# Linear attention on one core: the orders of loads, stores and first and last heads, rewritten by hand

## The chip, the cores and the metric

The kernel runs on one core of one Trainium2 chip. The metric is the device time of one execution in microseconds (us). A kernel's time is the median of its runs. One execution more was taken with the hardware profiler; its span runs from the first to the last instruction on the core, and its device time is a little longer than that span.

## The reference

32 heads, each with q, k and v of 2048 rows by 128 columns in bf16. phi(x) is x + 1 where x > 0 and exp(x) elsewhere; the kernel computes it as max(x, 0) + min(exp(x), 1), with the small constant added to the second term.

```python
phi_q = jnp.where(q > 0, q + 1, jnp.exp(q)) + 1e-6
phi_k = jnp.where(k > 0, k + 1, jnp.exp(k)) + 1e-6
kv  = jnp.einsum("bhsd,bhse->bhde", phi_k, v)
z   = jnp.einsum("bhsd->bhd", phi_k)
num = jnp.einsum("bhqd,bhde->bhqe", phi_q, kv)
den = jnp.einsum("bhqd,bhd->bhq", phi_q, z)[..., None] + 1e-6
return num / den
```

q, k and v are 16.8 MB each and the output is as large again, so the core moves 67 MB through its DMA engines.

## The kernel before

**Tiles.** A head is loaded as three transfers of 512 KB (q, k, v) and stored as one of 512 KB. Row p*16 + j of a head lies in partition p at place j, so that each tensor of a head is a tile of 128 partitions by 16 blocks of 128 columns. There are 7 buffers for each of k, q and v (`NI`), 12 for the output (`NO`) and 2 for every intermediate tile.

**The steps of a head h, with the names that the order lists use.** A number after the dot is the part of a step that is cut (the first head's are cut in halves, the last head's q steps in three).

- `ldk`, `ldq`, `ldv` (lines 367 and 372): the loads. They are issued by SP, but for `ldv0.0`, which ScalarE issues. A load of head h waits until the tile of head h - 7 has been used.
- `ek` (L384, ScalarE): exp of k. `em` (L387, VectorE): its minimum with 1. `rkp` (L394, GpSimd) and for the first head `rkd` (L390, VectorE): max(k, 0). `v1` (L398, GpSimd): v copied beside a column of ones.
- `kv` (L405, TensorE): 32 matmuls that add up phi(k)^T [v, 1] in PSUM. `kvs` (L410, VectorE): the sum copied to SBUF.
- `T` (L417, TensorE): 16 transposes of q into PSUM. They need the PSUM tile free: `eq`, `rqa` and `rqb` of the head before.
- `eq` (L421) and `rqa` (L427) on ScalarE, `emq` (L423) and `rqb` (L430) on VectorE: phi of the transposed q.
- `n` (L441, L446, L448, TensorE): phi(q) times the copied sum, 12 blocks as `n.0` and 4 as `n.1` (6, 6 and 4 for the last head).
- `a` (L461), `r` (L464), `f` (L468, VectorE): the denominator plus its constant, its reciprocal, the product into the output tile. `f.0` is the big one, `f.1` the small one.
- `st` (L477, SP): the store, which waits for all `f` of its head. For the three heads in `FEW` (line 64) it is cut by rows instead: 96 partitions as an ordinary store (L351), the other 32 as pieces whose outermost dimension is 4 or 3 (L356).
- `w` (L339, TensorE): matmuls on the identity whose result nobody reads, 28 in all at the start.

**What sets the order.** Nothing is scheduled at run time. `ORDER` (line 105) lists for each of PE, DVE, ACT, POOL and SP the names of its steps in the order in which that engine runs them. `Program.resolve` turns the dependences into waits on semaphores. An engine does one step after the other, and a step that has to wait holds up everything behind it in its list. That holds for SP's list too: it is one line of loads and stores, all in one DMA queue, and a store whose `f` is not ready keeps the loads behind it from being issued.

In the line before, 25 loads of SP's list (places 0 to 24, counted from zero) stand ahead of the first store `st0.0`; with `ldv0.0` these are 26. From there on stores stand among the loads, and `st18.0` to `st31.2` stand behind the last load `ldq31.0`.

Of the kernel before, what the change touches and what calls it, by code (L numbers as in the profile page):

```python
# [57 lines left out]
def groups(h):  # L58
    if h == NH - 1:
        return ((0, 2, 3, 0), (6, 2, 3, 2), (12, 2, 2, 4))  # L60
    return ((0, 4, 3, 0), (12, 2, 2, 4))


FEW = {4: ((0, 96, 16), (96, 120, 3), (120, 128, 4)), 8: ((0, 96, 16), (96, 128, 4)), 17: ((0, 96, 16), (96, 128, 4))}


def st_rows(h, i):
    return FEW[h][i] if h in FEW else (0, P, 16)

# [34 lines left out]

ORDER = {
    "PE": """
        w16 w2 w0 w6 w7 kv0.0 w8 w5 T0.0 w9 w4 T0.1 w10 w11 w12 w13 w1 kv0.1 w14 w15 w3 T1.0 kv1.0 n0.0 n0.1
        T2.0 kv2.0 n1.0 T3.0 n1.1 kv3.0 n2.0 T4.0 n2.1 kv4.0 n3.0 T5.0 n3.1 kv5.0 n4.0 T6.0 n4.1 kv6.0 n5.0 T7.0
        n5.1 kv7.0 n6.0 T8.0 n6.1 kv8.0 n7.0 T9.0 n7.1 kv9.0 n8.0 T10.0 n8.1 kv10.0 n9.0 T11.0 n9.1 kv11.0 n10.0
        T12.0 n10.1 kv12.0 n11.0 T13.0 n11.1 kv13.0 n12.0 T14.0 n12.1 kv14.0 n13.0 T15.0 n13.1 kv15.0 n14.0  # L110
        T16.0 n14.1 kv16.0 n15.0 T17.0 n15.1 kv17.0 n16.0 T18.0 n16.1 kv18.0 n17.0 T19.0 n17.1 kv19.0 n18.0
        T20.0 n18.1 kv20.0 n19.0 T21.0 n19.1 kv21.0 n20.0 T22.0 n20.1 kv22.0 n21.0 T23.0 n21.1 kv23.0 n22.0
        T24.0 n22.1 kv24.0 n23.0 T25.0 n23.1 kv25.0 n24.0 T26.0 n24.1 kv26.0 n25.0 T27.0 n25.1 kv27.0 n26.0
        T28.0 n26.1 kv28.0 n27.0 T29.0 n27.1 kv29.0 n28.0 T30.0 n28.1 kv30.0 n29.0 T31.0 T31.1 n29.1 kv31.0
        n30.0 n30.1 n31.0 n31.1 n31.2
    """,
    "DVE": """
        ones eps0 em0.0 rkd0.0 v1ones0 em0.1 v1ones1 eps1 em1.0 emq0.0 rqb0.0 kvs0 emq0.1 eps2 em2.0 kvs1 rqb1.0
        r0.0 f0.0 emq1.0 em3.0 a0.1 kvs2 r0.1 rqb2.0 f0.1 r1.0 f1.0 emq2.0 em4.0 a1.1 r1.1 rqb3.0 f1.1 r2.0 kvs3
        f2.0 emq3.0 em5.0 a2.1 kvs4 r2.1 rqb4.0 f2.1 r3.0 f3.0 emq4.0 em6.0 a3.1 r3.1 rqb5.0 f3.1 r4.0 kvs5 f4.0  # L120
        emq5.0 em7.0 a4.1 r4.1 rqb6.0 f4.1 r5.0 kvs6 f5.0 emq6.0 em8.0 a5.1 r5.1 rqb7.0 f5.1 r6.0 kvs7 f6.0
        emq7.0 em9.0 a6.1 r6.1 rqb8.0 f6.1 r7.0 kvs8 f7.0 emq8.0 em10.0 a7.1 r7.1 rqb9.0 f7.1 r8.0 kvs9 f8.0
        emq9.0 em11.0 a8.1 r8.1 rqb10.0 f8.1 r9.0 kvs10 f9.0 emq10.0 em12.0 a9.1 r9.1 rqb11.0 f9.1 r10.0 kvs11
# [54 lines left out]
class Program:  # L178
# [84 lines left out]
def bass_standalone__linear_attn_elu__prompt_kernel(nc: bass.Bass, q: bass.AP, k: bass.AP, v: bass.AP, out: bass.AP):  # L263
# [11 lines left out]
    with ExitStack() as es:  # L275
# [99 lines left out]
        def head(h):  # L375
# [99 lines left out]
            for i, (a, b) in enumerate(st_parts(h)):  # L475
                add("SP", f"st{h}.{i}", lambda e, a=a, b=b, i=i: some(
                    e, o_sb[:, h % NO], of[h], *st_rows(h, i)) if h in FEW else e.dma_start(rows(of, h)[:, a:b], o_sb[:, h % NO, a:b]),  # L477
                    [f"f{h}.{j}" for j, (t0, nb, m, b0) in enumerate(groups(h)) if t0 < b and a < t0 + nb * m],
# [44 lines left out]
```

## Time and profile before

| What | Value |
|---|---|
| median of 3 runs | 169.07 us (168.45 to 169.11) |
| the profiled execution | 168.74 us |
| its span | 167.4 us |
| mean granted TensorE clock | 0.997 |
| TensorE, VectorE, ScalarE, GpSimd busy | 94%, 92%, 89%, 56% of the span |
| bytes read and written in HBM | 50.33 MB, 16.78 MB |

The table gives whole-span shares. The engines' shares are far from full only at both ends of the span; between 26 and 146 us TensorE, VectorE and ScalarE are all nearly without a gap, and so is the DMA.

### The profile page before, as it was taken

The numbers are of one execution on the slowest core, as the hardware profiler recorded it, in microseconds if no ns is written. First come the engines' busy times: TensorE is split into PE (matmuls) and PEld (weight loads), VectorE is DVE, ScalarE is ACT, GpSimd is POOL, SyncE is SP. The second block draws the span as 40 slices with busy tenths as digits, with TensorE's granted clock in tenths as the row PEclk, the third lists the DMA queues.
The fourth block names the chain that finished last, engine by engine and source line by source line (L and its number), as shares of the span: only waits on it lengthen the run. The fifth ranks groups of instructions, "written<-read, shape, count | busy, mean of one in ns | idle before, by whom it ended". The sixth has DMA issues, their size and how long they took to land.

```text
span 167.4 us, 6190 instructions
## 1 busy us (share of the span) xinstructions
PE 156.7 (94%) x2716; PEld 151.2 (90%) x2716; DVE 154.4 (92%) x300; ACT 149.5 (89%) x102; POOL 94.1 (56%) x71
## 2 busy tenths in 40 slices
PE   6999969999999999999999999999999999999740
PEld 2579859999999999999999999999999999999640
DVE  0389999999999999999999999999999999999990
ACT  4899949999999999999999999999999999995700
POOL 2779646656656666655555566666555555670000
PEclk9999999999999999999999999999999999999998
DMA  5999999999999999999999999999999999999995
GB/s 206 432 423 419 395 423 388 419 409 415 411 419 407 407 427 411 417 395 421 415 389 425 418 414 420 426 407 423 402 442 390 425 416 428 405 409 415 414 376 226
DMA packets 9834, 67.51 MB, mean 403 GB/s; under 512 B 2095, under 2 KB 2479, under 8 KB 6831
## 3 DMA queue, kind: packets, MB, share of 16 engines
q1 hardware_dynamic: 9663, 66.59, 97.3%
q8 instruction: 21, 0.34, 0.8%
q10 hardware_dynamic: 144, 0.52, 0.8%
q14 instruction: 6, 0.05, 0.1%
HBM read 50.33 MB, written 16.78 MB: 401 GB/s over the span
## 4 chain that ended last, share of the span: by engine, by line
PE 88%; DVE 8%; issue 0%; POOL 0%; POOLq 0%
PE la L405 34%; PE la L446 17%; PE la L417 17%; PE la L448 16%; PE la L339 5%; DVE la L468 4%; DVE la L387 1%; DVE la L423 1%; DVE la L464 1%; DVE la L430 0%; PE la L441 0%; DVE la L461 0%; DVE la L410 0%; POOL la L324 0%; POOL la L323 0%
## 5 line engine op out<-in xcount | busy, mean ns | idle before, releaser
L394 POOL TENSOR_SCALAR la<-la 128x2048 bf16<-128x2048 bf16 (+1 forms) x32 | 60.5, 1892 | 49.9 <-PE la L405 46.6
L468 DVE TENSOR_TENSOR la<-la 128x1536 bf16<-128x1536 f32 (+2 forms) x65 | 77.7, 1196 | 0.2
L446 PE MATMUL la<-la 128*128 128x129 bf16 x512 | 67.0, 219 | 0.1
L448 PE MATMUL la<-la 128*128 128x129 bf16 x512 | 67.0, 219 | 0.0
L421 ACT ACTIVATE la<-la 128x2048 bf16<-128x2048 bf16 (+2 forms) x35 | 60.2, 1730 | 5.3 <-PE la L448 4.0
L384 ACT ACTIVATE la<-la 128x2048 bf16<-128x2048 bf16 (+1 forms) x33 | 61.3, 1860 | 2.5 <-DMA la<-in_k_dram 2.5
L405 PE MATMUL la<-la 128*128 128x129 bf16 x1024 | 63.4, 220 | 0.0
L405 PEld LDWEIGHTS la<-la 128*128 128x128 bf16 x1024 | 59.5, 98 | 0.4
L448 PEld LDWEIGHTS la<-la 128*128 128x128 bf16 x512 | 49.5, 97 | 0.0
L446 PEld LDWEIGHTS la<-la 128*128 128x128 bf16 x512 | 47.9, 97 | 0.3 <-DVE la L410 0.3
L398 POOL COPY la<-la 128x1024 int32<-128x1024 int32 (+1 forms) x33 | 34.4, 1042 | 5.4 <-PE la L405 3.4
L417 PE MATMUL la<-la 128*128 128x128 bf16 x512 | 34.0, 219 | 1.6 <-DVE la L430 1.6
L427 ACT ACTIVATE la<-la 128x1024 bf16<-128x1024 bf16 (+1 forms) x32 | 33.5, 1047 | 0.0
L417 PEld LDWEIGHTS la<-la 128*128 128x128 bf16 x512 | 30.0, 98 | 2.4 <-DVE la L430 1.8
L387 DVE TENSOR_SCALAR la<-la 128x2048 bf16<-128x2048 bf16 (+1 forms) x33 | 24.8, 751 | 6.1 <-ACT la L384 6.1
L423 DVE TENSOR_SCALAR la<-la 128x2048 bf16<-128x2048 bf16 (+2 forms) x35 | 25.1, 717 | 0.3 <-ACT la L421 0.3
L441 PE MATMUL la<-la 128*128 128x3 bf16 (+1 forms) x128 | 21.6, 169 | 1.8 <-DVE la L468 1.4
L430 DVE TENSOR_SCALAR la<-la 128x1024 bf16<-128x1024 bf16 x31 | 20.5, 661 | 0.0
L441 PEld LDWEIGHTS la<-la 128*128 128x128 bf16 x128 | 12.5, 97 | 2.1 <-DVE la L468 1.5
L464 DVE RECIPROCAL la<-la 128x12 f32<-128x12 f32 (+2 forms) x65 | 12.9, 200 | 1.3 <-PE la L448 0.3
L339 PE MATMUL la<-la 128*128 128x480 bf16 x28 | 8.8, 464 | 1.5 <-POOL la L324 1.5
L410 DVE CAST la<-la 128x129 bf16<-128x129 f32 x32 | 7.8, 244 | 0.1
(16 smaller groups left out, 11.9 us busy)
## 6 DMA issues: line engine op xcount, KB each, us to landing
la<-in_k_dram SPq DMA_DIRECT2D x32, 512.0 KB, 19.2
la<-in_q_dram SPq DMA_DIRECT2D x32, 512.0 KB, 19.6
la<-in_v_dram SPq DMA_DIRECT2D x31, 512.0 KB, 19.4
out_dram<-la SPq DMA_DIRECT2D x28, 512.0 KB, 19.2
out_dram<-la SPq DMA_DIRECT2D x3, 384.0 KB
la<-in_v_dram ACTq DMA_DIRECT2D x1, 512.0 KB, 4.3
out_dram<-la SPq DMA_DIRECT2D x3, 128.0 KB, 3.8
out_dram<-la SPq DMA_DIRECT2D x2, 192.0 KB, 3.4
```

The costliest lines, as they stand in the source:

```text
L384: add("ACT", f"ek{h}.{i}", lambda e, a=a, b=b: e.activation(em_sb[:, h % NE, a:b], k_sb[:, h % NI, a:b], ACT.Exp), over("ldk", h, ld_parts ...
L394: add("POOL", f"rkp{h}.{i}", lambda e, a=a, b=b: e.tensor_scalar(rk_sb[:, h % NR, a:b], k_sb[:, h % NI, a:b], BIG, 0.0, op0=ALU.min, op1=A ...
L398: add("POOL", f"v1{h}.{i}", lambda e, a=a, b=b: e.tensor_copy(v1_sb[:, h % NV, a:b, 0:D].bitcast(i32), v_sb[:, h % NI, a:b].bitcast(i32)), ...
L405: ins = e.matmul(kv_ps, lhsT=src[:, j], rhs=v1_sb[:, h % NV, j, 0:NC], start=(j + part == 0), stop=(j == NT - 1 and part == 1))
L417: ins = e.transpose(xT[:, j], q_sb[:, h % NI, j], ident[:])
L421: add("ACT", f"eq{h}.{i}", lambda e, a=a, b=b: e.activation(emq_sb[:, h % NQ, a:b], xT[:, a:b], ACT.Exp), over("T", h, t_parts, a, b) + fr ...
L423: add("DVE", f"emq{h}.{i}", lambda e, a=a, b=b: e.tensor_scalar(emq_sb[:, h % NQ, a:b], emq_sb[:, h % NQ, a:b], 1.0, EPS, op0=ALU.min, op1 ...
L427: add("ACT", f"rqa{h}", lambda e: e.activation(rq_sb[:, h % NQ, 0:n], xT[:, 0:n], ACT.Relu), over("T", h, t_parts, 0, n) + freed(NQ, h, (" ...
L441: e.matmul(_ap(o_ps[:, :], o + D, [[NC, m]]), lhsT=ones[:], rhs=epsr[:, 0:m], start=True, stop=False, skip_group_check=True)
L446: e.matmul(to, lhsT=emq_sb[:, h % NQ, t], rhs=kvs_sb[:, h % NK, 0:NC], start=late and c == 0, stop=False, skip_group_check=True)
L448: ins = e.matmul(to, lhsT=rq_sb[:, h % NQ, t], rhs=kvs_sb[:, h % NK, 0:NC], start=False, stop=True, skip_group_check=True)
L468: return e.tensor_tensor(out=_ap(o_sb[:, :, :, :], first(o_sb[:, h % NO, t0, 0:1]) - first(o_sb[:, :, :, :]), [[m * D, nb], [D, m], [1, D] ...
```

## The change

Only `FEW` and the lists in `ORDER` are edited. Every step stays, with its size and its engine; the waits between steps are worked out anew from the new order.

- **SP.** `ldq5.0` and `ldk6.0` change places, and `st0.0` now stands at place 18, right behind 18 loads. Stores then stand among the loads at an even pace. Where before `st0` to `st17` stood ahead of the last load, now `st0` to `st20` do, and 11 stores stand behind it where there were 14.
- **Pieces.** The stores cut by rows are those of heads 0, 2 and 5 instead of 4, 8 and 17. The cuts are the same: one head in 96 + 24 + 8 partitions, two heads in 96 + 32.
- **TensorE.** At the start 22 `w` matmuls stand ahead of `T0.0`, one between `T0.0` and `T0.1`, then both halves of `kv0`, then 5 more `w`. At the end `kv31.0` stands ahead of `n29.1`, `T31.0` and `T31.1`.
- **VectorE.** Some small steps of the first heads move (`emq1.0` goes ahead of `f0.0`; `kvs2` and `kvs4` come later), and the last six heads are ordered anew (`emq29.0` behind `f28.0`, `rqb30.0` behind `f28.1`, `emq30.0` behind `f29.0`, the parts of `emq31` and `kvs31`).
- **ScalarE.** `rqa30` goes ahead of `eq30.0`, and `rqa31` ahead of `eq31.2`.
- **GpSimd.** `rkp27.0` goes ahead of `v127.0`, `v128.0` ahead of `rkp28.0`, `rkp29.0` ahead of `v129.0`.

```diff
-FEW = {4: ((0, 96, 16), (96, 120, 3), (120, 128, 4)), 8: ((0, 96, 16), (96, 128, 4)), 17: ((0, 96, 16), (96, 128, 4))}
+FEW = {0: ((0, 96, 16), (96, 128, 4)), 2: ((0, 96, 16), (96, 128, 4)), 5: ((0, 96, 16), (96, 120, 3), (120, 128, 4))}
...
     "PE": """
-        w16 w2 w0 w6 w7 kv0.0 w8 w5 T0.0 w9 w4 T0.1 w10 w11 w12 w13 w1 kv0.1 w14 w15 w3 T1.0 kv1.0 n0.0 n0.1
+        w16 w5 w6 w7 w2 w8 w4 w9 w1 w0 w10 T0.0 w11 T0.1 kv0.0 kv0.1 w12 w13 w3 w14 w15 T1.0 kv1.0 n0.0 n0.1
...
-        T28.0 n26.1 kv28.0 n27.0 T29.0 n27.1 kv29.0 n28.0 T30.0 n28.1 kv30.0 n29.0 T31.0 T31.1 n29.1 kv31.0
+        T28.0 n26.1 kv28.0 n27.0 T29.0 n27.1 kv29.0 n28.0 T30.0 n28.1 kv30.0 n29.0 kv31.0 n29.1 T31.0 T31.1
         n30.0 n30.1 n31.0 n31.1 n31.2
     "DVE": """
-        ones eps0 em0.0 rkd0.0 v1ones0 em0.1 v1ones1 eps1 em1.0 emq0.0 rqb0.0 kvs0 emq0.1 eps2 em2.0 kvs1 rqb1.0
-        r0.0 f0.0 emq1.0 em3.0 a0.1 kvs2 r0.1 rqb2.0 f0.1 r1.0 f1.0 emq2.0 em4.0 a1.1 r1.1 rqb3.0 f1.1 r2.0 kvs3
-        f2.0 emq3.0 em5.0 a2.1 kvs4 r2.1 rqb4.0 f2.1 r3.0 f3.0 emq4.0 em6.0 a3.1 r3.1 rqb5.0 f3.1 r4.0 kvs5 f4.0
+        ones rkd0.0 em0.0 eps0 v1ones0 v1ones1 em0.1 em1.0 emq0.0 eps1 rqb0.0 kvs0 emq0.1 eps2 em2.0 kvs1 rqb1.0
+        r0.0 emq1.0 f0.0 em3.0 a0.1 r0.1 rqb2.0 f0.1 r1.0 kvs2 f1.0 emq2.0 em4.0 a1.1 r1.1 rqb3.0 f1.1 r2.0 kvs3
+        f2.0 emq3.0 em5.0 a2.1 r2.1 rqb4.0 f2.1 r3.0 kvs4 f3.0 emq4.0 em6.0 a3.1 r3.1 rqb5.0 f3.1 r4.0 kvs5 f4.0
...
-        f24.0 emq25.0 em27.0 a24.1 r24.1 rqb26.0 f24.1 r25.0 kvs26 f25.0 emq26.0 em28.0 a25.1 r25.1 rqb27.0
-        f25.1 r26.0 kvs27 f26.0 emq27.0 em29.0 a26.1 r26.1 rqb28.0 f26.1 r27.0 kvs28 f27.0 emq28.0 em30.0 a27.1
-        r27.1 rqb29.0 f27.1 kvs29 r28.0 emq29.0 f28.0 em31.0 a28.1 rqb30.0 r28.1 kvs30 f28.1 r29.0 emq30.0 f29.0
-        emq31.0 a29.1 r29.1 f29.1 emq31.1 kvs31 r30.0 emq31.2 f30.0 a30.1 r30.1 f30.1 r31.0 f31.0 a31.1 r31.1
-        r31.2 f31.1 f31.2
+        f24.0 emq25.0 em27.0 a24.1 r24.1 rqb26.0 f24.1 r25.0 kvs26 f25.0 emq26.0 em28.0 a25.1 kvs27 r25.1
+        rqb27.0 f25.1 r26.0 f26.0 emq27.0 em29.0 a26.1 r26.1 rqb28.0 f26.1 r27.0 kvs28 f27.0 emq28.0 em30.0
+        a27.1 r27.1 rqb29.0 f27.1 r28.0 kvs29 f28.0 emq29.0 em31.0 a28.1 r28.1 kvs30 f28.1 rqb30.0 r29.0 f29.0
+        emq30.0 a29.1 kvs31 r29.1 f29.1 emq31.0 emq31.1 r30.0 f30.0 a30.1 r30.1 emq31.2 f30.1 r31.0 f31.0 a31.1
+        r31.1 r31.2 f31.1 f31.2
     "ACT": """
...
-        eq30.0 rqa30 eq31.0 eq31.1 eq31.2 rqa31
+        rqa30 eq30.0 eq31.0 eq31.1 rqa31 eq31.2
     "POOL": """
...
-        rkp21.0 v121.0 rkp22.0 v122.0 rkp23.0 v123.0 rkp24.0 v124.0 rkp25.0 v125.0 rkp26.0 v126.0 v127.0 rkp27.0
-        rkp28.0 v128.0 v129.0 rkp29.0 rkp30.0 v130.0 rkp31.0 v131.0
+        rkp21.0 v121.0 rkp22.0 v122.0 rkp23.0 v123.0 rkp24.0 v124.0 rkp25.0 v125.0 rkp26.0 v126.0 rkp27.0 v127.0
+        v128.0 rkp28.0 rkp29.0 v129.0 rkp30.0 v130.0 rkp31.0 v131.0
     "SP": """
         ldk0.0 ldk1.0 ldq0.0 ldv1.0 ldk2.0 ldq1.0 ldv2.0 ldk3.0 ldq2.0 ldv3.0 ldk4.0 ldq3.0 ldv4.0 ldq4.0 ldk5.0
-        ldv5.0 ldk6.0 ldq5.0 ldv6.0 ldk7.0 ldv7.0 ldv8.0 ldq6.0 ldk8.0 ldq7.0 st0.0 ldv9.0 ldk9.0 ldq8.0 ldv10.0
-        ldk10.0 st1.0 ldk11.0 ldq9.0 ldk12.0 ldq10.0 ldk13.0 ldv11.0 ldq11.0 ldv12.0 ldq12.0 st2.0 ldv13.0
-        ldv14.0 st3.0 ldv15.0 ldk14.0 ldq13.0 st4.0 ldq14.0 ldk15.0 st4.1 ldv16.0 ldk16.0 ldk17.0 ldq15.0
...
-        ldv27.0 st12.0 ldq27.0 ldv28.0 ldk28.0 st13.0 ldv29.0 ldq28.0 ldk29.0 st14.0 ldq29.0 ldk30.0 st15.0
-        ldv30.0 ldk31.0 ldq30.0 st16.0 ldv31.0 st17.0 st17.1 ldq31.0 st18.0 st19.0 st20.0 st21.0 st22.0 st23.0
+        ldv5.0 ldq5.0 ldk6.0 st0.0 ldv6.0 ldk7.0 ldk8.0 ldq6.0 ldv7.0 st0.1 ldq7.0 ldv8.0 ldq8.0 ldk9.0 ldv9.0
+        st1.0 ldk10.0 ldk11.0 ldv10.0 ldq9.0 st2.0 ldv11.0 ldq10.0 ldk12.0 ldv12.0 ldq11.0 st2.1 ldq12.0 ldv13.0
+        ldk13.0 ldv14.0 ldk14.0 st3.0 ldv15.0 ldq13.0 ldv16.0 ldk15.0 st4.0 ldq14.0 ldk16.0 ldk17.0 st5.0
+        ldq15.0 st5.1 ldq16.0 st5.2 ldv17.0 ldq17.0 ldk18.0 ldq18.0 ldv18.0 st6.0 ldk19.0 ldv19.0 ldq19.0
...
+        st12.0 ldq26.0 st13.0 ldv27.0 ldk28.0 ldv28.0 ldq27.0 st14.0 ldq28.0 st15.0 ldk29.0 ldv29.0 ldk30.0
+        ldv30.0 ldq29.0 st16.0 st17.0 ldk31.0 ldq30.0 ldv31.0 st18.0 st19.0 st20.0 ldq31.0 st21.0 st22.0 st23.0
         st24.0 st25.0 st26.0 st27.0 st28.0 st29.0 st30.0 st31.0 st31.1 st31.2
```

More of the change, by code (lines that the diff above doesn't have):

```diff
@@ L155 @@
         ldk0.0 ldk1.0 ldq0.0 ldv1.0 ldk2.0 ldq1.0 ldv2.0 ldk3.0 ldq2.0 ldv3.0 ldk4.0 ldq3.0 ldv4.0 ldq4.0 ldk5.0
-        ldv5.0 ldk6.0 ldq5.0 ldv6.0 ldk7.0 ldv7.0 ldv8.0 ldq6.0 ldk8.0 ldq7.0 st0.0 ldv9.0 ldk9.0 ldq8.0 ldv10.0
-        ldk10.0 st1.0 ldk11.0 ldq9.0 ldk12.0 ldq10.0 ldk13.0 ldv11.0 ldq11.0 ldv12.0 ldq12.0 st2.0 ldv13.0
-        ldv14.0 st3.0 ldv15.0 ldk14.0 ldq13.0 st4.0 ldq14.0 ldk15.0 st4.1 ldv16.0 ldk16.0 ldk17.0 ldq15.0
-        ldk18.0 ldq16.0 ldq17.0 ldv17.0 ldk19.0 st4.2 ldq18.0 ldq19.0 ldv18.0 ldv19.0 ldk20.0 st5.0 ldv20.0
-        ldk21.0 st6.0 ldq20.0 ldk22.0 ldq21.0 ldv21.0 ldk23.0 st7.0 ldv22.0 ldk24.0 st8.0 ldq22.0 ldv23.0 st8.1
-        ldv24.0 ldv25.0 ldq23.0 st9.0 ldq24.0 ldq25.0 ldk25.0 st10.0 ldk26.0 ldk27.0 ldq26.0 st11.0 ldv26.0
-        ldv27.0 st12.0 ldq27.0 ldv28.0 ldk28.0 st13.0 ldv29.0 ldq28.0 ldk29.0 st14.0 ldq29.0 ldk30.0 st15.0
-        ldv30.0 ldk31.0 ldq30.0 st16.0 ldv31.0 st17.0 st17.1 ldq31.0 st18.0 st19.0 st20.0 st21.0 st22.0 st23.0
+        ldv5.0 ldq5.0 ldk6.0 st0.0 ldv6.0 ldk7.0 ldk8.0 ldq6.0 ldv7.0 st0.1 ldq7.0 ldv8.0 ldq8.0 ldk9.0 ldv9.0
+        st1.0 ldk10.0 ldk11.0 ldv10.0 ldq9.0 st2.0 ldv11.0 ldq10.0 ldk12.0 ldv12.0 ldq11.0 st2.1 ldq12.0 ldv13.0
+        ldk13.0 ldv14.0 ldk14.0 st3.0 ldv15.0 ldq13.0 ldv16.0 ldk15.0 st4.0 ldq14.0 ldk16.0 ldk17.0 st5.0
+        ldq15.0 st5.1 ldq16.0 st5.2 ldv17.0 ldq17.0 ldk18.0 ldq18.0 ldv18.0 st6.0 ldk19.0 ldv19.0 ldq19.0
+        ldk20.0 st7.0 ldv20.0 ldq20.0 ldk21.0 ldk22.0 st8.0 ldv21.0 ldk23.0 ldq21.0 ldv22.0 st9.0 ldv23.0
+        ldq22.0 ldq23.0 ldq24.0 st10.0 ldk24.0 ldv24.0 ldk25.0 ldk26.0 st11.0 ldv25.0 ldq25.0 ldk27.0 ldv26.0
+        st12.0 ldq26.0 st13.0 ldv27.0 ldk28.0 ldv28.0 ldq27.0 st14.0 ldq28.0 st15.0 ldk29.0 ldv29.0 ldk30.0
+        ldv30.0 ldq29.0 st16.0 st17.0 ldk31.0 ldq30.0 ldv31.0 st18.0 st19.0 st20.0 ldq31.0 st21.0 st22.0 st23.0
         st24.0 st25.0 st26.0 st27.0 st28.0 st29.0 st30.0 st31.0 st31.1 st31.2
```

## The prediction

> **What bounds the kernel now.** I read the page first, then busy time by stretches, the waits, the chain of work that ended last, and the timelines of SP and VectorE at both ends. The page, in shares of the span:
>
> ```profile
> span 167.4 us, 6190 instructions
> ...
> DMA  5999999999999999999999999999999999999995
> ...
> q1 hardware_dynamic: 9663, 66.59, 97.3%
> ```
>
> The queue of loads and stores alone fills 97.3% of the 16 DMA engines' time, and only the first and the last slice are not full. By stretches (busy time per engine, granted clock, DMA share, GB/s):
>
> ```profile
> 4.00:26.00 22.00, 20.03 (x280) 16.58 (x279) 18.02 (x27) 18.70 (x14) 14.71 (x11) 1.00 1.02 416
> 26.00:58.00 32.00, 32.00 (x585) 31.97 (x583) 31.76 (x64) 31.75 (x22) 20.69 (x14) 1.00 1.01 410
> 58.00:90.00 32.00, 32.00 (x586) 32.00 (x583) 31.76 (x64) 31.78 (x22) 20.13 (x14) 1.00 1.02 414
> 90.00:130.00 40.00, 40.00 (x732) 40.00 (x730) 39.69 (x81) 39.75 (x27) 24.66 (x18) 1.00 1.01 416
> 130.00:146.00 16.00, 16.00 (x294) 16.00 (x292) 15.90 (x31) 15.88 (x11) 9.89 (x7) 1.00 1.01 416
> 146.00:160.00 14.00, 12.49 (x227) 12.15 (x225) 13.55 (x31) 10.13 (x9) 3.33 (x2) 1.00 1.01 410
> 160.00:167.00 7.00, 1.67 (x32) 1.50 (x29) 3.53 (x8) 0.00 (x0) 0.00 (x0) 0.97 0.79 313
> ```
>
> The DMA runs at 410 to 416 GB/s from 4 to 160 us, whether only loads are in it (4 to 26), loads and stores, or almost only stores (146 to 160). One transfer of 512 KB (524288 bytes) takes 524288/414 = 1.27 us at that rate. From 26 to 146 TensorE, VectorE and ScalarE are full too. Here the waits from 26 to 150 us, all of them, and two steps of the chain:
>
> ```profile
> POOL la L394 <- PE la L405: 44.9, 25, 3.5
> POOL la L398 <- PE la L405: 3.4, 2, 1.7
> ACT la L421 <- PE la L448: 2.2, 1, 2.2
> ```
>
> ```profile
> 140.32 1.81 PE la L405 x32
> ...
> 144.94 1.81 PE la L405 x32
> ```
>
> Nobody waits for a load; a head takes 144.94 - 140.32 = 4.62 us on TensorE. Two things thus run side by side, the compute at its own pace and the DMA at its own, and which of them ends last is seen at the end: SP's last four stores, and what SP waited for after 160 us.
>
> ```profile
> 160.56 3.40 SPq L477 DMA_DIRECT2D out_dram<-la  x4
> ```
>
> ```profile
> SPq L494 <- DMA out_dram<-la: 3.1, 2, 2.2
> ```
>
> The last store is issued at 163.96 and the span ends 3.4 us later. How long would it take if nothing were queued ahead of it? The first load went into an empty queue:
>
> ```profile
> 0.73 0.40 SPq L372 DMA_DIRECT2D la<-in_k_dram  x1
> ...
> 3.97 2.00 ACT L384 ACTIVATE la<-la 128x1024 bf16<-128x1024 bf16 x2 [1.74 <-DMA la<-in_k_dram]
> ```
>
> From issue to use are 3.24 us for 512 KB. The last store is 128 KB, so three quarters of 1.27 us go: 2.3 us. The other 1.1 us are transfers still queued. **The DMA bounds the end, and the compute may end up to 1.1 us later for nothing.** An earlier end of compute gains at most what the DMA leaves idle.
>
> **The change part by part.** Bytes, transfers and cuts of pieces stay, so the DMA's busy time stays. It can end earlier or later only if it idles less or more, or if the compute passes it by over 1.1 us.
>
> *Does the queue run dry at `st0.0`?* SP around it:
>
> ```profile
> 15.85 0.65 SPq L367 DMA_DIRECT2D la<-in_q_dram  x1
> 23.83 0.35 SPq L477 DMA_DIRECT2D out_dram<-la  x1
> 24.23 0.94 SPq L367 DMA_DIRECT2D la<-in_v_dram  x1
> ```
>
> SP stands until 23.83, when `f0.1` is done. Before, 26 loads are queued then; after, 19. At 4.0 one has landed; 416 GB/s over 22 us are 9.15 MB or 17.5 more, 18.5 by 26.0, so the nineteenth ends at 26.0 + 0.5 x 1.27 = 26.6. A store issued into an empty queue needs 3.24 - 1.27 = 2.0 us around its transfer; issued by 24.6 it follows without a hole. `f0.1` leaves 0.8 us. Behind it SP issues loads in at most 0.94 us each, less than 1.27, so the queue fills again. Cost: nothing, covered by the queued loads. Is `f0.1` still as early?
>
> ```profile
> 18.48 1.51 DVE L423 TENSOR_SCALAR la<-la 128x2048 bf16<-128x2048 bf16 x1
> 19.90 2.37 DVE L387 TENSOR_SCALAR la<-la 128x2048 bf16<-128x2048 bf16 x1
> ...
> 22.27 0.28 DVE L410 CAST la<-la 128x129 bf16<-128x129 f32 x1
> ...
> 22.55 0.66 DVE L430 TENSOR_SCALAR la<-la 128x1024 bf16<-128x1024 bf16 x1
> 23.13 0.68 DVE L468 TENSOR_TENSOR la<-la 128x512 bf16<-128x512 f32 x1
> ```
>
> These are `emq1.0`, `em3.0`, `kvs2`, `rqb2.0`, `f0.1`; the page's groups give the means of the lines of `em` and of `rqa`:
>
> ```profile
> L427 ACT ACTIVATE la<-la 128x1024 bf16<-128x1024 bf16 (+1 forms) x32 | 33.5, 1047 | 0.0
> L387 DVE TENSOR_SCALAR la<-la 128x2048 bf16<-128x2048 bf16 (+1 forms) x33 | 24.8, 751 | 6.1 <-ACT la L384 6.1
> ```
>
> After, `emq1.0` and `f0.0` swap, their sum stays, and `kvs2` leaves the way of `rqb2.0`: all behind it is 22.55 - 22.27 = 0.2 to 0.3 us earlier, and `T3.0`, which needs `rqb2.0`, with it. The unknown is how long the bf16 steps take at this place: `em3.0` has 2.37 us here and a mean of 0.75, and `emq1.0`, as large, has 1.51. So `f0.1` lies between 1.6 us earlier (`em3.0` at its mean) and 0.9 later (`emq1.0` as long as `em3.0`). I take 0.2 earlier, nearest to the row as it stands.
>
> *The first heads on TensorE.* The same 28 `w` and the same 96 transposes and matmuls of heads 0 and 1 stand ahead of `n0.0`, in another order. I take 0; a stall of up to 0.5 us would be under the same cover of 1.1.
>
> *Do the loads still come in time?* Now three more stores stand ahead of `ldq31.0`: it is transfer 117 in units of 512 KB (96 loads, 21 stores), before 114. The stretches add up to 1 + 17.5 + 25.0 + 25.3 + 31.7 + 12.7 = 113.2 by 146.0, so it lands at 146.0 + 3.8 x 1.28 = 150.9 on an average DMA engine, 3.8 later than before. It is used by `T31.0`:
>
> ```profile
> 152.83 0.89 PE la L417 x16
> 154.18 1.83 PE la L405 x32
> ```
>
> The first row is `T31`, the second `kv31`; the 0.46 between them is `n29.1`. After, `kv31` and `n29.1` stand ahead of `T31`: 152.83 + 1.83 + 0.46 = 155.1. Slack 4.2. The other tight loads by the same sum, `ldv29.0` (transfer 105), `ldk31.0` (111), `ldq30.0` (112) and `ldv31.0` (113), land at 135.7, 143.2, 144.5 and 145.8 on average. Their uses, `v129`, `rkp31`, `T30` and `v131`, in the same order, with `rkp29` second:
>
> ```profile
> 137.58 1.04 POOL L398 COPY la<-la 128x1024 int32<-128x1024 int32 x1 [1.72 <-PE la L405]
> 138.58 1.89 POOL L394 TENSOR_SCALAR la<-la 128x2048 bf16<-128x2048 bf16 x1
> ...
> 146.84 1.89 POOL L394 TENSOR_SCALAR la<-la 128x2048 bf16<-128x2048 bf16 x1 [1.74 <-PE la L405]
> 148.68 1.49 POOL L398 COPY la<-la 128x1024 int32<-128x1024 int32 x1
> ```
>
> ```profile
> 148.21 0.89 PE la L417 x16
> ```
>
> Slacks are 1.9, 3.6, 3.7 and 2.9. But `rkp29` goes ahead of `v129` now, so `v129` starts at 137.58 + 1.89 = 139.5, and `kv29` wants it only at 144.94. A load counts when its slowest DMA engine is done, and this lag shows where somebody waited for a load:
>
> ```profile
> 18.40 1.04 POOL L398 COPY la<-la 128x1024 int32<-128x1024 int32 x1 [1.22 <-DMA la<-in_v_dram]
> ```
>
> `ldv3.0` is the eleventh transfer, on average at 16.6 by the sum; it was used at 18.4: lag 1.8 us. The slacks, 2.9 and more, cover that. Cost: nothing.
>
> *The tail on VectorE.* From `f29.0` on:
>
> ```profile
> 153.68 1.74 DVE L468 TENSOR_TENSOR la<-la 128x1536 bf16<-128x1536 f32 x1
> ...
> 156.03 0.16 DVE L461 TENSOR_SCALAR la<-la 128x4 f32<-128x4 f32 x1 [0.28 <-PE la L405]
> ...
> 157.78 1.75 DVE L468 TENSOR_TENSOR la<-la 128x1536 bf16<-128x1536 f32 x1
> ```
>
> From `f29.0` (153.68) to the last `f` VectorE has one gap, 0.28 at `a29.1`, which waits for `kv31`. After, `kv31` is 1.4 earlier and the gap goes; `emq31.2` moves behind `f30.0`, as `rqa31` (2048 wide, some 1.9 where 1024 take 1.05) now runs ahead of `eq31.2`: +0.15 on the last `f`. Net between -0.3 and +0.3, I take 0; hidden by 1.1.
>
> **Sum:** span 167.4 + 0 (dry queue) + 0 (loads) + 0 (compute -0.2 at the start and 0 in the tail, both hidden) = 167.4. The profiled execution took 168.74, 1.3 more than its span, and lies 0.33 below the median 169.07. Forecast 168.7, its own range 168.0 to 169.4.
>
> **The rivals.** A measurement here can tell about 0.5% (0.85 us) from no change.
>
> *Late loads (slower).* Pieces with an outermost dimension of 4 or 3 cannot use all 16 DMA engines alike. Were they always to fall on the same few, those carry 8 + 8 + 8 rows from the pieces and 2 more by head 5's last one, 26 above the others, by place 60 instead of place 115. A row of 4 KB at 414/16 GB/s takes 0.158 us, so they end 4.1 us behind, and with the 1.8 measured 5.9. Then `ldq30.0` lands at 144.5 + 5.9 = 150.4, 2.2 after its use; less 1.1 of cover the end moves by 1.1: **169.8**. It decides from a lag of 3.7 + 1.1 = 4.8 on. For it: the DMA share of 0.79 in the last 7 us, some engines ending earlier than others. Against it: the same pieces were all in the queue by then before, too, and nobody waited. The Trainium skill, "DMA: Bandwidth & Descriptors", section "Why a DMA increments its semaphore by 16 and not by 1", says that the engine count is the largest number up to 16 that divides the slowest dimensions, and that hardware queues use the lowest-numbered ones; by that rule the same few it is, whereas no row here shows which engine took what.
>
> *Dry queue (slower).* If `f0.1` comes 0.9 later, 24.7, the hole is 0.1; if another 1.5 comes on top (`emq1.0` doubled), 1.6: up to 170.3; the middle is **169.6**.
>
> *Filled tail (faster).* 0.21 x 7 = 1.5 us of an average engine's time is idle in the last stretch. If the new order fed those engines earlier, up to 1.5 would go; two thirds of it give **167.7**. Against it: VectorE's last `f` is no earlier by more than some tenths.
>
> *No effect of the order at all*, that is, SP standing at the stores as long as before for want of room in the queue, gives the forecast's time.
>
> **How the numbers follow.** Forecast, with the last rival: 0.56. Late loads 0.20, dry queue 0.08, filled tail 0.16. Faster 0.16, same 0.56, slower 0.28. The range reaches to both neighbours: from 167.7 (the filled tail) to 170.2 (late loads with 0.4 more lag).
>
> **What would show it.** Right: DMA slices full from the second to the last but one, `st0.0` issued at 23.3 to 24.0, no wait for a load after 26 us, the last store's issue within 0.4 of 163.96. Late loads: ScalarE, GpSimd or TensorE waiting for a DMA after 100 us, and an end of compute beyond 165. Dry queue: a DMA slice at 26 to 30 us below 9. The forecast is wrong if the GB/s between 26 and 146 move, since it takes them as fixed.

## The result, and the profile after

| What | Before | After |
|---|---|---|
| median | 168.93 us (16 runs, 168.45 to 169.22) | 168.28 us (16 runs, 168.17 to 169.02) |
| the profiled execution, its span | 168.74, 167.4 us | 168.94, 167.6 us |
| profiled once more (`after_again` below) | | 168.25, 166.9 us |

The ratio after to before is 0.9972 [0.9958, 0.9985]: a gain of 0.3%. Its interval does not reach 1, but it lies inside the half per cent that the prediction counted as no change.

The first profiled execution of after lies 0.66 us above its own median. Its span, DMA slices and queue, from its page of the profile:

```profile
span 167.6 us, 6190 instructions
...
DMA  5999999999999999999999999999999999999995
...
q1 hardware_dynamic: 9663, 66.59, 96.9%
```

Two stretches show where (in each row: the stretch and its length, busy time of PE, PEld, DVE, ACT and POOL, granted clock, DMA share, GB/s; a share of 1.01 is read as full):

```profile
4.00:26.00 22.00, 21.23 (x316) 18.22 (x315) 17.24 (x33) 20.44 (x16) 15.07 (x12) 1.00 1.02 406
26.00:90.00 64.00, 63.64 (x1156) 63.44 (x1154) 63.55 (x124) 63.01 (x42) 40.37 (x28) 1.00 1.01 415
```

Its first 22 us, with only loads in the queue, ran at 406 GB/s where before had 416: 10/416 of 22 us, 0.5 us lost before any store. The second profiled execution of the same kernel started at 415, so that is no property of the change. I therefore read the second one, by the stretches that the prediction used:

```profile
4.00:26.00 22.00, 22.00 (x324) 18.93 (x323) 17.99 (x34) 21.06 (x16) 16.20 (x12) 1.00 1.02 415
26.00:58.00 32.00, 32.00 (x585) 32.00 (x583) 31.76 (x64) 31.77 (x22) 20.54 (x15) 1.00 1.01 414
58.00:90.00 32.00, 31.78 (x574) 31.49 (x572) 31.37 (x63) 31.22 (x21) 19.21 (x15) 1.00 1.01 415
90.00:130.00 40.00, 40.00 (x730) 40.00 (x728) 39.72 (x78) 39.72 (x27) 25.57 (x18) 1.00 1.01 417
130.00:146.00 16.00, 15.92 (x290) 15.75 (x288) 15.86 (x32) 15.65 (x11) 9.43 (x7) 1.00 1.02 421
146.00:160.00 14.00, 12.21 (x222) 11.89 (x219) 13.70 (x29) 8.57 (x8) 2.53 (x2) 1.00 1.00 405
160.00:167.00 7.00, 0.38 (x8) 0.20 (x5) 2.27 (x6) 0.00 (x0) 0.00 (x0) 0.71 0.73 287
```

Against before's rows in the prediction the DMA is faster in four stretches: 414 for 410, 415 for 414, 417 for 416, 421 for 416. Times their lengths these are (4 x 32 + 1 x 32 + 1 x 40 + 5 x 16) KB = 0.28 MB, or 0.68 us at 414 GB/s; the slower first stretch takes back 1 x 22 KB. At 146 us after is thus 0.6 us of transfers ahead. From 146 to 160 us it is slower, 405 for 410 at a share of 1.00, which takes back 5 x 14 = 70 KB or 0.2 us; in the last stretch less is left to do. That leaves some 0.45 us, and the spans differ by 0.5. Up to 146 us the DMA share is as full as before, 1.01 to 1.02: no idle time was filled, **the transfers themselves were faster**.

SP's stores at the end, its first store, and the waits for loads from 26 to 150 us (waited in total, times, longest):

```profile
159.32 3.35 SPq L477 DMA_DIRECT2D out_dram<-la  x4
```

```profile
21.47 0.37 SPq L351 DMA_DIRECT2D out_dram<-la  x1
```

```profile
POOL la L394 <- DMA la<-in_k_dram: 8.8, 4, 2.9
POOL la L398 <- DMA la<-in_v_dram: 1.1, 3, 0.5
```

The last store is issued at 162.67, 1.3 earlier than before, and 4.2 us pass to the end of the span instead of 3.4. The first store is issued 2.4 us earlier. And GpSimd now does wait for loads, 9.9 us in all, where before nobody did.

### The profile page after: what moved, and what is told of

The parts are those of the page before. It is cut to its first block, busy times and chain, and to the rows that moved or that the text cites. A ratio compares the mean times of both kernels' runs of the same rounds, so it can differ in the third digit from the quotient of the medians.

```text
span 167.6 us, 6190 instructions
## 1 busy us (share of the span) xinstructions
PE 156.3 (93%) x2716; PEld 150.9 (90%) x2716; DVE 153.6 (92%) x300; ACT 149.5 (89%) x102; POOL 93.9 (56%) x71
## 4 chain that ended last, share of the span: by engine, by line
DVE 80%; PE 11%; DMA 4%; issue 2%; SPq 1%
DVE la L468 40%; DVE la L423 11%; DVE la L387 10%; DVE la L430 10%; DVE la L464 5%; PE la L405 4%; DMA la<-in_q_dram 4%; DVE la L410 3%; PE la L417 2%; DVE la L461 2%; PE la L446 2%; PE la L448 2%; PE la L339 1%; SPq L367 0%; SPq L372 0%
## 5 line engine op out<-in xcount | busy, mean ns | idle before, releaser
L387 DVE TENSOR_SCALAR la<-la 128x2048 bf16<-128x2048 bf16 (+1 forms) x33 | 23.3, 705 | 4.1 <-ACT la L384 4.0
L423 DVE TENSOR_SCALAR la<-la 128x2048 bf16<-128x2048 bf16 (+2 forms) x35 | 26.1, 745 | 0.0
L339 PE MATMUL la<-la 128*128 128x480 bf16 x28 | 7.9, 440 | 1.5 <-POOL la L324 1.5
```

The lines of the kernel that those rows point to most:

```text
L387: add("DVE", f"em{h}.{i}", lambda e, a=a, b=b: e.tensor_scalar(em_sb[:, h % NE, a:b], em_sb[:, h % NE, a:b], 1.0, EPS, op0=ALU.min, op1=AL ...
L423: add("DVE", f"emq{h}.{i}", lambda e, a=a, b=b: e.tensor_scalar(emq_sb[:, h % NQ, a:b], emq_sb[:, h % NQ, a:b], 1.0, EPS, op0=ALU.min, op1 ...
```

## The experiments

Three theories stood at the start; the expectations number them. **DMA** (theory 1): only what is in the one queue, and when, counts. **Compute** (theory 2): the new orders of the heads end the compute earlier or later, and that is the time. **Pieces** (theory 3): the new places of the cut stores make the gain. All ratios are to the kernel before, with their 95% intervals; spans, stretches and rows are of the one profiled execution of each.

**compute_new.** Before, with the changed lists of TensorE, VectorE, ScalarE and GpSimd; SP's line and `FEW` stay.

```diff
 FEW, "SP": as before
-"PE", "DVE", "ACT", "POOL": as before
+"PE", "DVE", "ACT", "POOL": as after
```

> The kernel before with the changed kernel's lists for TensorE, VectorE, ScalarE and GpSimd; SP's line and the pieces stay as before. Theory 1 (the DMA line sets the end, the order of the compute is hidden): ratio to before 1.000, within 0.1%, although the compute ends earlier. Theory 2 (the compute, ahead by 1.6 us at head 5 in the changed kernel's profile, hands the last stores over earlier and fills the tail): 0.997. Theory 3 (the places of the pieces): 1.000.

1.0001 [0.9982, 1.0019]. SP's stores at its end:

```profile
155.01 7.75 SPq L477 DMA_DIRECT2D out_dram<-la  x5
```

The last store goes out at 162.76, 1.2 us earlier than before, and the span is 167.7: nothing is gained. An earlier end of the compute is worth nothing while before's line of transfers stays, as theory 1 had it.

**sp_new.** The other half: before, with after's SP line and `FEW`.

```diff
-FEW, "SP": as before
+FEW, "SP": as after
 "PE", "DVE", "ACT", "POOL": as before
```

> The kernel before with the changed kernel's line for SP and its pieces (heads 0, 2 and 5); the compute lists stay as before. Theory 1 (the new line of loads and stores alone makes the gain): 0.997. Theory 2 (the earlier compute makes it): 1.000, or slower by up to 0.5%, as the last loads come later for an order of steps that wants them earlier. Theory 3 (the places of the pieces): 0.997.

0.9987 [0.9967, 1.0006], between before and after and told apart from neither, so the time decides between no two theories. The stretch from 26 to 90 us, first of before, then of sp_new, and sp_new's stores at the end:

```profile
26.00:90.00 64.00, 64.00 (x1167) 63.97 (x1165) 63.52 (x126) 63.53 (x43) 40.82 (x28) 1.00 1.01 412
```

```profile
26.00:90.00 64.00, 63.84 (x1159) 63.61 (x1157) 63.28 (x125) 63.12 (x42) 39.17 (x29) 1.00 1.01 415
```

```profile
154.35 10.73 SPq L477 DMA_DIRECT2D out_dram<-la  x6
```

The DMA is as fast as in after, 415 where before has 412, but the last store is issued only at 165.08, 2.3 us from the end. That is the time estimated for a last store with nothing queued ahead of it: here the compute ends last.

**pieces_old, no_pieces, pieces_late, pieces_012.** After, with the cut stores at heads 4, 8, 17; with none; at heads 16, 17, 18; at heads 0, 1, 2. The pieces' places in SP's line go with them. Two more theories come in with the last two expectations. Theory R: pieces put the DMA engines out of step, so that some store while others load, and packets of loads get shorter by that. Theory L: the new line alone makes the gain. In these diffs C2 stands for ((0, 96, 16), (96, 128, 4)) and C3 for ((0, 96, 16), (96, 120, 3), (120, 128, 4)).

```diff
-FEW = {0: C2, 2: C2, 5: C3}
+FEW = {4: C3, 8: C2, 17: C2}     # pieces_old
+FEW = {}                         # no_pieces
+FEW = {16: C2, 17: C2, 18: C3}   # pieces_late
+FEW = {0: C2, 1: C2, 2: C3}      # pieces_012
```

> The changed kernel with its pieces back at heads 4, 8 and 17 (the same cuts, at such places of the new line that they follow their heads as before). Theory 3 (early pieces make the gain): the gain goes, 1.000. Theories 1 and 2: it stays, 0.997.

> The changed kernel with whole stores only, no piece anywhere. If the last DMA engines set the end and the pieces take rows off them, this is slower than the changed kernel: 26 rows of 0.158 us on the few against 6 fewer on each of the others, so about 6 x 0.158 = 0.9 us or 0.5%: ratio to before 1.002 to 1.003. If the compute sets the end, it stays at 0.997.

> The changed kernel with the same three cuts at heads 16, 17 and 18, the last before the last load. Rows of each DMA engine in all are those of the changed kernel. Theory R: the gain goes, 0.2 to 0.3% slower than the changed kernel, 0.999 to 1.001, with 26 to 90 us at the rate of the kernel without pieces. Theory L, or only the sum of rows of each engine counts: 0.997.

> The changed kernel with the same three cuts at heads 0, 1 and 2, the earliest possible. Theory R: as fast as the changed kernel or 0.1% faster, 0.996 to 0.997, with 26 to 58 us at 415 GB/s or more. Theory L: 0.997. If the changed kernel's own three heads were a lucky fit to the instruction fetches: slower, 1.000.

1.0006 [0.9985, 1.0028], 1.0055 [1.0038, 1.0072], 1.0022 [1.001, 1.0035] and 0.9984 [0.9971, 0.9996]. The stretch from 26 to 90 us of each, in this order:

```profile
26.00:90.00 64.00, 63.54 (x1156) 63.40 (x1153) 63.02 (x124) 62.94 (x42) 39.52 (x28) 1.00 1.01 413
```

```profile
26.00:90.00 64.00, 62.24 (x1122) 61.65 (x1120) 62.23 (x120) 61.14 (x41) 39.19 (x28) 1.00 1.01 411
```

```profile
26.00:90.00 64.00, 63.15 (x1149) 63.00 (x1147) 62.62 (x122) 62.55 (x41) 39.35 (x28) 1.00 1.01 412
```

```profile
26.00:90.00 64.00, 63.53 (x1142) 62.78 (x1140) 62.84 (x122) 62.27 (x41) 40.23 (x28) 1.00 1.01 415
```

With the new line alone nothing is gained, against theory L; with early pieces the rate is 415 and the time falls. The pieces count twice: where they stand, and that they are there at all (0.8% between none and after). Two sizes were missed: no pieces cost twice what was expected (1.002 to 1.003), and pieces_012 gained half (0.996 to 0.997). Why is not shown.

**early_in_old.** Before's line and compute, only the pieces at heads 0, 2, 5.

```diff
-FEW = {4: C3, 8: C2, 17: C2}
+FEW = {0: C2, 2: C2, 5: C3}
 "SP": loads and st*.0 as before
```

> The kernel before with one thing changed: its pieces are of heads 0, 2 and 5, each placed in the old line a few transfers behind its head's store. Theory R (pieces put the DMA engines out of step, so that some store while others load, and load packets get shorter; the earlier, the longer this works): ratio to before 0.998, and the GB/s from 26 to 90 us rise by 2 or 3. Theory L (the new line, with stores from place 18 on, makes the gain, the pieces none): 1.000.

0.9994 [0.9985, 1.0003]: no change that can be told.

```profile
26.00:90.00 64.00, 64.00 (x1168) 64.00 (x1165) 63.51 (x126) 63.57 (x42) 39.56 (x29) 1.00 1.01 412
```

Pieces of early heads alone do not raise the rate either. But in the old line they are not as early in time. The pieces' rows (L356: shortest, median and longest ns at SP, first and last start), early_in_old, then after_again:

```profile
L356 SPq DMA_DIRECT2D out_dram<-la x4: 792/1122/2118, 23.5 to 76.4; - x4
```

```profile
L356 SPq DMA_DIRECT2D out_dram<-la x4: 790/942/1083, 25.3 to 60.0; - x4
```

The last piece goes out 16 us later than in after_again. So it takes both parts of the change as they are; that the new line does more than bring the pieces forward is not shown.

**dry.** After, with `st0.0` ahead of `ldq4.0`, behind 13 loads instead of 18, to price a hole in the queue.

```diff
-... ldv4.0 ldq4.0 ldk5.0 ldv5.0 ldq5.0 ldk6.0 st0.0 ldv6.0
+... ldv4.0 st0.0 ldq4.0 ldk5.0 ldv5.0 ldq5.0 ldk6.0 ldv6.0
```

> The changed kernel with the first store at place 13 instead of 18, so that 14 transfers are queued when SP stands at it. They end at 20.4 us on average, the store's data are ready at 21.7 and it needs 1 to 2 us to begin: a hole of 2.3 to 3.3 us in the DMA. No step wants a load earlier than it then lands by more than some tenths. If the DMA line sets the end: 2.3 to 3.3 us slower than the changed kernel, ratio to before 1.011 to 1.017. If the compute sets it: 0.997 to 1.000.

1.022 [1.0203, 1.0237], 172.47 us, 4.2 above after. Its DMA slices, its first store, and three stretches:

```profile
DMA  5999679999999999999999999999999999999995
```

```profile
21.97 0.37 SPq L351 DMA_DIRECT2D out_dram<-la  x1
```

```profile
4.00:18.00 14.00, 13.02 (x165) 9.97 (x164) 9.32 (x18) 12.36 (x10) 10.66 (x9) 1.00 1.03 417
18.00:24.00 6.00, 6.00 (x112) 6.00 (x110) 5.96 (x11) 6.00 (x5) 3.98 (x3) 1.00 0.52 178
24.00:30.00 6.00, 4.30 (x79) 4.15 (x77) 5.05 (x10) 2.64 (x3) 0.63 (x1) 1.00 1.01 339
```

The last two stretches in after_again:

```profile
18.00:24.00 6.00, 6.00 (x111) 5.95 (x109) 5.97 (x11) 5.95 (x4) 4.16 (x3) 1.00 1.03 418
24.00:30.00 6.00, 6.00 (x115) 6.00 (x113) 5.93 (x14) 5.97 (x6) 3.93 (x3) 1.00 1.02 415
```

The hole is 6 x (1 - 0.52) = 2.9 us of idle DMA. The loss in bytes is larger: 178 for 418 GB/s over 6 us are 3.4 us, and the stretch behind it, with a full share but only 339 for 415, another 1.1. These 4.5 us compare with 4.6 between the two spans (171.5 and 166.9). The expectation, 1.011 to 1.017, had only the hole. The loads behind it came late too, and TensorE lost 3.5 of the 32 us from 26 to 58. Still it is not the compute that ends last: the last store goes out at 167.4, 4.1 us before the end, against 2.3 in sp_new. A DMA that idles early is paid for in full, and more, at the end: the DMA theory.

**after_again, old_start, old_tail, four_cuts.** After itself; after with before's order of TensorE and VectorE up to head 15; after with before's order from head 15 on, ScalarE and GpSimd too; after with one more cut store.

```diff
+"PE" up to kv15.0, "DVE" up to kvs15: as before      # old_start
+"PE" from kv15.0, "DVE" from kvs15, "ACT", "POOL": as before   # old_tail
+FEW = {0: C2, 2: C2, 5: C3, 7: C2}, st7.1 behind ldv20.0     # four_cuts
```

> The changed kernel once more, on the same chip as the next three, as their anchor: ratio to before 0.996 to 0.9985, and 414 to 416 GB/s from 26 to 90 us as in its first profile, whether or not its start is as slow as in that one (406 GB/s from 4 to 26 us).

> The changed kernel with the old order of the first heads on TensorE and VectorE, the rest as changed. The compute then starts as late as before (about 2 us at head 5). Theory R with the DMA setting the end: 0.997 to 0.998, since 415 GB/s stay and the later compute is under the cover of what the last store waits for; the first store comes at 23.8 instead of 21.7, still ahead of the end of the queue. If the earlier compute is part of the gain: 0.999 to 1.000.

> The changed kernel with the old order of the last heads on all four compute engines, the start as changed. Last loads come as late as in the changed kernel, for an order that wants them earlier (T31.0 ahead of kv31.0). If the new tail is what carries the late loads: 0.998 to 1.000, as with all compute lists old (0.9987), with waits for loads at 135 us and later. If the cover holds: 0.997.

> The changed kernel with a fourth store in 96 + 32 partitions, of head 7: four DMA engines carry 8 rows more against the others (1.3 us), the other twelve 2 rows less (0.3 us). Without any cut the time was 1.0055. If the twelve still end last: 0.1 to 0.2% faster than the changed kernel, 0.995 to 0.996. If the four end last by now: 0.3 to 0.6% slower than it, 1.000 to 1.003.

0.9965 [0.9953, 0.9977], 0.997 [0.9959, 0.9981], 0.9968 [0.9955, 0.998] and 1.0014 [1.0001, 1.0027]. Neither half of the new compute order, left out alone, costs anything; the fourth cut gives all of the gain back. In four_cuts the DMA is as fast as in after_again, but SP's last stores are late:

```profile
26.00:90.00 64.00, 63.51 (x1150) 63.12 (x1148) 63.07 (x124) 62.66 (x42) 39.27 (x29) 1.00 1.01 414
```

```profile
153.93 11.31 SPq L477 DMA_DIRECT2D out_dram<-la  x6
```

The last one goes out at 165.24, 2.5 us from the end. What made it late is seen where GpSimd, ScalarE and VectorE meet (start, us, step):

```profile
137.93 1.90 POOL L394 TENSOR_SCALAR la<-la 128x2048 bf16<-128x2048 bf16 x1 [3.04 <-PE la L448]
139.76 1.04 POOL L398 COPY la<-la 128x1024 int32<-128x1024 int32 x1
141.14 1.96 POOL L394 TENSOR_SCALAR la<-la 128x2048 bf16<-128x2048 bf16 x1 [0.34 <-PE la L405]
```

```profile
137.86 1.91 ACT L384 ACTIVATE la<-la 128x2048 bf16<-128x2048 bf16 x1 [0.42 <-DMA la<-in_k_dram]
```

```profile
140.10 1.25 DVE L423 TENSOR_SCALAR la<-la 128x2048 bf16<-128x2048 bf16 x1
141.27 2.38 DVE L387 TENSOR_SCALAR la<-la 128x2048 bf16<-128x2048 bf16 x1
```

GpSimd stood for 3.04 us; the row puts that down to a matmul, but ScalarE, which needs a k tile too, waited for its load until 137.86, within 0.1 us of GpSimd's start, so I read both as one late load of k. The landings in the trace bear it out. The trace has sixteen landings for every load, which I take for one of each DMA engine; those of this load come at 134.86 on average and at 137.78 at last, in after_again at 134.72 and 136.77. The fourth cut thus left the average engine where it was and made the slowest 1.0 us later. GpSimd's three steps then ran that much later and beside VectorE's two bf16 steps, which took 1.25 and 2.38 instead of 0.68 each: 2.3 us lost on VectorE. In after_again the same load is late by 2.88, but there VectorE's second step starts 0.15 us *before* GpSimd's, takes 0.68, and GpSimd's takes the longer time:

```profile
140.26 0.68 DVE L387 TENSOR_SCALAR la<-la 128x2048 bf16<-128x2048 bf16 x1
```

```profile
136.92 1.89 POOL L394 TENSOR_SCALAR la<-la 128x2048 bf16<-128x2048 bf16 x1 [2.88 <-DMA la<-in_k_dram]
...
140.41 2.29 POOL L394 TENSOR_SCALAR la<-la 128x2048 bf16<-128x2048 bf16 x1 [0.61 <-PE la L405]
```

This is the upper time that was expected (1.000 to 1.003), but not for the reason given there, that the four engines with more rows end last: the sixteen landings of the last store lie within 1.0 us of each other in four_cuts as in after_again.

The kernels side by side, without dry, whose hole reaches into the stretch. The bytes are summed from the trace's packets in the loads' and stores' queue between 26 and 90 us; the last column is the longest bf16 step of 2048 columns on VectorE (L387 or L423) after 100 us, in the profiled execution.

| Kernel | Line of stores | Cut heads | MB, 26 to 90 us | Last store, then to the end, us | Longest bf16 step, us |
|---|---|---|---|---|---|
| before | old | 4, 8, 17 | 26.18 | 163.96, 3.4 | 0.7 |
| compute_new | old | 4, 8, 17 | 26.15 | 162.76, 4.9 | 0.7 |
| early_in_old | old | 0, 2, 5 | 26.19 | 162.24, 5.0 | 0.7 |
| no_pieces | new | none | 26.19 | 164.67, 4.0 | 1.27 |
| pieces_late | new | 16, 17, 18 | 26.23 | 165.67, 3.0 | 2.37 |
| pieces_old | new | 4, 8, 17 | 26.26 | 164.11, 4.2 | 1.32 |
| old_start | new | 0, 2, 5 | 26.34 | 162.94, 4.2 | 1.14 |
| four_cuts | new | 0, 2, 5, 7 | 26.35 | 165.24, 2.5 | 2.38 |
| pieces_012 | new | 0, 1, 2 | 26.36 | 163.45, 4.0 | 0.7 |
| after_again | new | 0, 2, 5 | 26.36 | 162.67, 4.2 | 1.14 |
| old_tail | new | 0, 2, 5 | 26.37 | 164.30, 2.6 | 2.37 |
| after | new | 0, 2, 5 | 26.38 | 163.60, 4.0 | 1.41 |
| sp_new | new | 0, 2, 5 | 26.41 | 165.08, 2.3 | 2.37 |

Two groups: up to 26.26 MB no kernel is faster than before, from 26.34 on all are, but sp_new, whose interval reaches 1.0006, and four_cuts. In these two the last store goes out latest of the second group, at 165.08 and 165.24, 2.3 and 2.5 us from the end; old_tail, with 164.30 and 2.6, is not slow. The means of the groups, 26.20 and 26.37, differ by 0.17 MB, 0.41 us at 414 GB/s, or 0.24%. The profiled executions of pieces_late and pieces_old took 170.02 and 169.63 us, 1.0 and 0.5 above the medians of these kernels, so their last two columns need not be typical.

## Why the prediction was right, and which term was mis-sized

**The signs.** Of the signs that the prediction named for being right, the full DMA slices came. The others did not: `st0.0` went out at 21.5 and not at 23.3 to 24.0, GpSimd waited for loads, and the last store went out at 162.67 (163.60 in the first profile, which would pass). The sign named for being wrong came as well: the GB/s between 26 and 146 us moved. The time stayed in the range because what this was worth, under half a per cent, was small.

**DMA sets the end, and compute may end later for nothing: right.** compute_new ends its compute 1.2 us earlier for nothing, old_tail 1.6 later than after_again (164.30 against 162.67) at no cost, and the hole of dry is paid in full. The 2.3 us estimated for an unloaded last store is what sp_new shows; no kernel has less. In after_again 4.2 us pass behind the last store's issue, so its cover is 1.9 us; sp_new and four_cuts use it up.

**Dry queue: the cost of nothing was right, the time of `f0.1` was not.** I took it 0.2 earlier and at most 1.6. It came 2.4 earlier in after_again (2.1 in after). VectorE and GpSimd of after_again there:

```profile
16.60 0.88 DVE L423 TENSOR_SCALAR la<-la 128x2048 bf16<-128x2048 bf16 x1
17.39 1.74 DVE L468 TENSOR_TENSOR la<-la 128x1536 bf16<-128x1536 f32 x1
19.06 0.93 DVE L387 TENSOR_SCALAR la<-la 128x2048 bf16<-128x2048 bf16 x1
...
20.76 0.68 DVE L468 TENSOR_TENSOR la<-la 128x512 bf16<-128x512 f32 x1
```

```profile
15.04 1.89 POOL L394 TENSOR_SCALAR la<-la 128x2048 bf16<-128x2048 bf16 x1 [0.66 <-PE la L405]
18.41 1.04 POOL L398 COPY la<-la 128x1024 int32<-128x1024 int32 x1 [1.48 <-DMA la<-in_v_dram]
```

and GpSimd of before (`rkp3`, then `rkp4`):

```profile
15.12 2.05 POOL L394 TENSOR_SCALAR la<-la 128x2048 bf16<-128x2048 bf16 x1 [0.25 <-PE la L405]
...
19.74 1.99 POOL L394 TENSOR_SCALAR la<-la 128x2048 bf16<-128x2048 bf16 x1 [0.31 <-PE la L405]
```

A bf16 step that starts while GpSimd is at work ends 0.54 to 0.55 us after GpSimd's step: before, `emq1.0` at 18.48 + 1.51 = 19.99 with `v13` done at 19.44, `em3.0` at 22.27 with `rkp4` done at 21.73; after, 17.48 with `rkp3` done at 16.93, and 19.99 with `v13` done at 19.45. The f32 product `f0.0` takes 1.74 to 1.76 beside either. After the swap each bf16 step meets only the end of a GpSimd step: that is 0.63 and 1.44 us of the 2.4, and the 0.3 predicted for `kvs2` are the rest. The Trainium skill, "SBUF — State Buffer", section "SBUF: two separate sides", says that VectorE's fast modes and GpSimd share a pair of ports under an exclusive lock, which the first to start holds for its whole instruction; these four ends agree with it. The prediction took the lengths of the bf16 steps for an unknown. They could have been read from before's rows: `rkp3` ends at 17.17, so `emq1.0`, put ahead of `f0.0`, had to end near 17.7 and not at 19.99, and `em3.0` to start before `rkp4`.

**First heads, and the tail: 0, right.** old_start (0.997) and old_tail (0.9968) are as fast as after.

**Loads in time: the cost was right, "no wait for a load after 26 us" was wrong.** From the trace's landings `ldq31.0` was there at 151.2 on the mean engine (predicted 150.9) and at 152.9 on the last: a lag of 1.7 where 1.8 was taken (2.5 in the first profile of after). But at `ldk22.0` the lag was already 2.6, and the compute, 2 us ahead since the first heads, reached the loads sooner. GpSimd waited; the compute fell back, and ended 1.3 us earlier instead of 2.4. That was covered. The rival *late loads* is thus a true mechanism with another price: not the lag alone, but 2.3 us on VectorE when GpSimd is pushed beside its bf16 steps. It ended sp_new and four_cuts; after_again is 0.15 us away from it. That pieces hit the same few engines is what the Trainium skill, "DMA: Bandwidth & Descriptors", section "Why a DMA increments its semaphore by 16 and not by 1", gives as a rule for hardware queues. The landings of `ldk22.0`, near 96 us, fit it: from the first of the sixteen to the last they spread over 3.0 to 4.0 us where at most one cut store was issued ahead of it (before, compute_new, no_pieces, pieces_late, pieces_old), over 4.6 to 5.4 behind three, and over 6.2 behind the four of four_cuts, whose mean is that of after_again (95.8 and 95.7). Which engine took what was not read. At `ldq31.0` the spread tells nothing: 5.0 and 6.1 us in the two profiles of after, 6.3 in four_cuts.

**The DMA's busy time: the mis-sized term.** "Bytes, transfers and cuts of pieces stay, so the DMA's busy time stays" took the GB/s as fixed. They rose in the stretch from 26 to 90 us, worth 0.4 to 0.5 us there. The sum gave 0 and 168.7; with this term it gives 168.2 to 168.3, and 168.28 was measured. So close a fit is partly luck: the 168.7 goes back to one execution, 0.2 below the median of before over 16 runs, and from that median the same term gives 168.4 to 168.5. It was not idle time filled at the end either (*filled tail*): the share in the last stretch is 0.73 after, 0.79 before.

What makes the transfers faster is only partly shown. Shown, by one profiled execution of each kernel and two of after, which agree within 0.02 MB: all kernels with the new line and early pieces move more bytes from 26 to 90 us than all others. The new line with later pieces or none has 26.19 to 26.26 MB, the old line with pieces at heads 0, 2, 5 has 26.19, before 26.18. The packet records agree. The 16-KB packets of loads that start between 26 and 90 us (those over 700 ns left out) take on average 631 to 632 ns in the old line, 628 to 629 in the new line with later pieces or none, and 624 to 626 in the new line with early pieces. Loads alone, from 16 to 26 us, take 636 to 639 in every kernel but dry; from 90 to 146 us all have 620 to 623.

Argued, not isolated: packets of loads are shorter where stores run beside them, and engines that are out of step mix the two sooner (theory R). The spread of the landings goes with the rate: for loads that land between 76 and 90 us it is 3.0 to 4.0 us on average in the first group of kernels and 4.6 to 4.8 in the second. Before 56 us it does not: 2.4 in no_pieces, 1.9 to 2.1 in after_again. early_in_old has 3.4 there, as its pieces went out later, so it does not refute theory R. A rival is thus left: that only the time at which the pieces go out counts, and the new line does no more than bring them forward. No run sent them out as early in the old line.

Open too is whether sp_new and after differ at all (their intervals overlap), and why no cuts cost 0.8%. no_pieces has moved as many bytes by 160 us as before, 64.39 MB, but its last store goes out 0.7 us later, and the sixteen landings of that store come at 167.57 on average and 168.61 at last, before's at 166.68 and 167.39. Of the 1.2 us, 0.9 are thus in the average engine and 0.3 in the slowest; what holds them back was not read.

## What to carry to other kernels

When one queue fills the whole span, ask of every edit two things: whether the queue ever idles, and whether the order of loads, stores and uneven pieces in it changes. The second moved the rate from 26 to 90 us by 0.6% here, 0.4 us, without a byte or a gap being removed. Do not take the GB/s as fixed when before's own stretches range from 410 to 416. And before costing a swap on VectorE, see which GpSimd step stands beside each bf16 step in the old and in the new order.

## What the runs showed of the hardware that was not expected

- A bf16 step of 128x2048 on VectorE takes 0.68 us alone and up to 2.38 when a GpSimd step has started first. In four_cuts one load for which GpSimd waited 3.04 us brought the longest one about; in after_again, with 2.88, it was missed by 0.15 us.
- A queue that had run dry for 2.9 us had a full DMA share again in the next 6 us, but 339 GB/s, where after_again has 415 at that time (dry).
- The same uneven pieces, moved to the first stores of the new line, changed the rate of the whole queue for 64 us: 413 GB/s in pieces_old, 414 and 415 in the two profiles of after.
- A fourth cut store left the average landing of a later load where it was and made its last landing 1.0 us later (four_cuts against after_again).
